# A causal attention and mixture-of-experts kernel: the router's embedding on ScalarE's queue, eleven warming transposes, some low parts on GpSimd, and a new order of steps

## Chip, core and metric

The kernel runs on one core of a Trainium2 chip. The time is the device time of one execution in microseconds (us), and lower is better.

## What is computed

Attention over 48 heads (4 batches of 12, 448 tokens, head width 64) is followed by a mixture of 8 experts on the 1792 tokens that it gives. Each token goes to the one expert with the largest logit.

```python
scores = scale * np.matmul(q, k.transpose(0, 1, 3, 2))
scores = np.where(mask, -1000000000.0, scores)          # causal
attn = softmax(scores); x = attn @ v                    # (4 x 448) x 768
en = expert_emb / (norm(expert_emb) + 1e-06)
logits = xn @ en.T / tau
expert_idx = np.argmax(logits, axis=1)
for e in range(8):
    h = np.maximum(x[mask_e] @ w1[e], 0.0)              # 768 -> 1024
    out[mask_e] = gate_w[mask_e] * (h @ w2[e])          # 1024 -> 768
```

## The kernel before

**Attention.** The heads are taken in 24 pairs (p = 0 to 23), six pairs to a batch. A pair's 448 rows are cut in four chunks of 112. For each pair TensorE makes the scores (steps S0 to S3, S02 for two chunks at once), VectorE masks each chunk and takes its row maximum (M, chunk and head, line 420), ScalarE takes the exponential (E, line 425), TensorE turns the result (T0, T2, T3, line 443), ScalarE or VectorE copies the turned blocks out of the accumulator banks (V0x to V3y, line 447), TensorE multiplies by v (PV0 to PV3), the result is copied (VO) and turned together with the router's product (X), and VectorE scales it into the token rows (XE) and the logits (LE). From pair 1 on GpSimd splits part of q and k into a high and a low part (hi, lo, lines 396 and 397), so that TensorE can use a faster format.

**The router's embedding.** Steps EE, es0 to esA load the embedding (8 x 768) and tau, square it (es0, ScalarE), and take the root by Newton steps on VectorE (es1 and following) to scale it.

**Routing.** After each batch of six pairs the steps R0 to Rc find every token's expert and rank, all on small tiles; q0 to qe sum the squares of the token rows on GpSimd. After batch 2 (pair 17) the most frequent expert, called star, is found (CN, Z0 to Z5, ZR), its w1 is loaded in six pieces (LW0 to LW5), each cast to a high part (W, ScalarE, line 603) and a low part (Wl, line 604: five on GpSimd, one on VectorE), and a first tile of its tokens is gathered (Y, YP, YI, YG).

**The experts.** After the last pair's X the first expert tile begins: F0 to F5 are its first product, HT turns its hidden row, G1 to G6 are part of its second product. Its w2 is loaded (LL), cast (A0 to A7, line 897) and its low parts taken (B0 to B7, line 898). Meanwhile the last batch's routing runs as one chain on VectorE: R0 to R5, R6, N0 to N9, Na to Nc give the place of each token in the expert tiles, TB is the product that collects it (line 942), IG writes the list, and GA gathers the second tile with it (line 626). That tile is turned by xta and xtb (line 672). Then a program of 128-token tiles (body) does the rest; TensorE runs it without a break.

**What sets the order.** One long string, ORDER, lists all attention, routing and first-tile steps. They are issued in that order, and each engine works through its own in that order; a token's `:k` names the bank, `/A`, `/V`, `/G` the engine (ScalarE, VectorE, GpSimd) for a step that may run on either.

Of the kernel before, what the change touches and what calls it, by code (L numbers as in the profile page):

```python
# [41 lines left out]
lo.1 E30.0 T3.0:0 E20.0 LDr.2 M00.0 hi.2 E11.0 M10.1 S02.1:2 M11.1 V3y.0/A V3x.0/V S3.1:1 LDv.0 E00.0 E01.0 E21.0
M01.1 M00.1 T0.0:0 lo.2 M21.1 E21.1 V0y.0/A M20.1 T2.0:2 M30.1 LDr.3 E20.1 V0x.0/A LDr.5 M31.1 V2y.0/V V2x.0/A S02.2:1
T2.1:0 S3.2:2 PV0.0:7 es1.0 E01.1 M31.2 V2y.1/A E31.1 E10.1 M20.2 PV1.0 V2x.1/A E11.1 S1.2:0 M30.2 E00.1 M10.2 PV2.0
M11.2 E30.1 hi.5 PV3.0 T0.1:2 M00.2 E30.2 M01.2 T3.1:0 M21.2 S1.3:1 LDv.1 LDr.4 LDr.6 V0y.1/A V0x.1/A es2.0 es3.0
V3y.1/V es4.0 M10.3 hi.3 V3x.1/A lo.3 S3.3:2 M11.3 es5.0 E31.2 S02.3:0 es6.0 M30.3 E01.2 hi.4 E20.2 T3.2:1 es7.0 M01.3
M20.3 es8.0 M31.3 lo.4 E11.2 PV0.1:6 PV1.1 V3x.2/A PV2.1 M21.3 PV3.1 RC.0/G E21.2 LDv.2 E00.2 es9.0:2 M00.3 E10.2
esA.0 T2.2:2 RC.1/G V3y.2/A VO.0/A T0.2:0 V2y.2/A V0y.2/A V2x.2/V S02.4:1 V0x.2/V LDr.7 X.0:2 M00.4 E01.3 M21.4 S3.4:0
PV0.2:7 E11.3 M01.4 E10.3 E20.3 E31.3 LE0.0 PV1.2 LDv.3 E30.3 LE1.0 XE1.0 M20.4 E00.3 E21.3 XE0.0 PV2.2 M30.4 M31.4
VO.1/V T3.3:1 RC.2/G lo.5 LDv.4 S1.4:0 V3y.3/V M11.4 M10.4 T0.3:2 PV3.2 V0y.3/V V3x.3/A S1.5:1 E20.4 V0x.3/A LDr.8  # L50
T2.3:0 S3.5:2 VO.2/A E21.4 V2y.3/A M10.5 E10.4 M11.5 E11.4 V2x.3/V M30.5 S02.5:1 M31.5 hi.6 lo.6 PV0.3:6 M21.5 M00.5
M01.5 X.1:2 E30.4 E00.4 M20.5 XE1.1 E11.5 E30.5 E01.4 T2.4:0 X.2:1 V2y.4/V LDv.5 E00.5 RC.3/G PV1.3 V2x.4/V XE1.2
LE1.2 E31.4 LE0.1 LDr.9 PV2.3 E01.5 LE0.2 XE0.1 E10.5 PV3.3 LE1.1 T0.4:0 XE0.2 V0x.4/A V0y.4/V T3.4:2 V3y.4/V V3x.4/A
S1.6:1 hi.8 M10.6 M11.6 S3.6:0 M31.6 S02.6:2 hi.7 E20.5 E21.5 M30.6 T0.5:1 PV0.4:7 M01.6 E31.5 M20.6 V0x.5/A M21.6
lo.7 T2.5:0 M00.6 V0y.5/A V2y.5/V T3.5:1 S02.7:2 RC.5/G VO.3/A V2x.5/A RC.4/G LDr.10 lo.8 V3x.5/A V3y.5/A S3.7:0 E01.6
M00.7 E30.6 M01.7 M21.7 E20.6 M20.7 M30.7 X.3:1 M31.7 LE1.3 XE1.3 S1.7:2 M11.7 XE0.3 PV1.4 PV2.4 PV3.4 E10.6 E11.6
LDv.6 E00.6 E21.6 M10.7 LE0.3 PV0.5:6 hi.9 T0.6:1 E31.6 V0y.6/A V0x.6/A LDr.11 VO.4/V T2.6:0 V2x.6/A X.4:2 V2y.6/V
E00.7 T3.6:1 E11.7 S02.8:0 PV1.5 E10.7 V3x.6/A E01.7 LDv.7 V3y.6/A PV2.5 lo.9 XE0.4 LE1.4 M00.8 M01.8 RC.6/G PV3.5
M20.8 XE1.4 LE0.4 E31.7 LDv.8 E00.8 S1.8:2 S3.8:1 M21.8 VO.5/V M11.8 X.5:0 M10.8 T0.7:2 XE1.5 PV0.6:7 E21.7 E21.8
LE0.5 hi.11 M31.8 E10.8 E20.7 PV1.6 E30.7 V0y.7/A LE1.5 V0x.7/V PV2.6 XE0.5 hi.10 E20.8 M30.8 PV3.6 T3.7:0 LDr.12  # L60
T2.7:2 VO.6/V V3x.7/A V3y.7/V V2y.7/A V2x.7/V S3.9:1 S02.9:0 M31.9 M30.9 E30.8 M01.9 E01.8 lo.10 S1.9:2 E31.8 q0.5
M11.9 E11.8 E01.9 PV0.7:7 hi.12 T3.8:1 M10.9 M21.9 X.6:2 R0.5:6 PV1.7 PV2.7 V3x.8/A V3y.8/A E30.9 PV3.7 XE0.6 RC.7/G
T0.8:1 M00.9 q3.5 q2.5 LE1.6 XE1.6 WX.5 q1.5 E31.9 LE0.6 M20.9 VO.7/A V0x.8/V LDr.13 T2.8:2 V0y.8/A V2x.8/A E11.9
E20.9 S3.10:0 V2y.8/V S02.10:1 E21.9 M30.10 M00.10 M01.10 LDv.10 E00.10 RC.8/G S1.10:2 PV0.8:7 M11.10 M31.10 M21.10
PV1.8 PV2.8 LDv.9 PV3.8 E00.9 lo.12 R1.5 E10.9 M20.10 T0.9:0 M10.10 R2.5 lo.11 R3.5 E21.10 S1.11:1 R4.5 X.7:2 M11.11
V0x.9/A LDr.14 qa1.5 M10.11 R5.5 V0y.9/A XE0.7 E30.10 T2.9:0 XE1.7 T3.9:1 V2x.9/A LE1.7 RK.5 LE0.7 V2y.9/A V3y.9/A
V3x.9/V VO.8/A E20.10 S02.11:2 S3.11:0 E31.10 RC.9/V X.8:1 M21.11 M30.11 E01.10 E11.10 M31.11 Rg.5/V hi.14 M01.11
qa0.5 PV0.9:7 M00.11 M20.11 E10.10 qb.5 PV1.9 PV2.9 E21.11 LE0.8 XE0.8 XE1.8 E01.11 T2.10:2 LE1.8 R6.5 E30.11 T0.10:0
V2y.10/V V0y.10/V T3.10:1 V2x.10/A S3.12:2 V3y.10/V V0x.10/A LDr.15 LDv.11 E00.11 M30.12 V3x.10/A S02.12:0 S1.12:1
R8.5 PV3.9 M20.12 E31.11 E11.11 PV0.10:6 M10.12 M11.12 M01.12 hi.13 E20.11 M00.12 qc.5 PV1.10 VO.9/A E10.11 M31.12  # L70
# [1111 lines left out]
```

## Time and profile before

| | us |
|---|---|
| median of 3 runs | 473.37 (473.09 to 474.11) |
| the profiled execution, its own time | 474.17 |
| span in its profile | 472.0 |
| busy: TensorE, VectorE, ScalarE, GpSimd | 454.4, 349.3, 295.9, 158.0 |

The busy time of TensorE is that of a pipelined engine whose ends are modelled, so 96% of the span does not say that TensorE sets the pace everywhere. The stretches up to about 161 us are attention, those behind it the experts.

### The profile page before, as it was taken

The numbers are of one execution on the slowest core, as the hardware profiler recorded it, in microseconds if no ns is written. First come the engines' busy times: TensorE is split into PE (matmuls) and PEld (weight loads), VectorE is DVE, ScalarE is ACT, GpSimd is POOL, SyncE is SP. The second block draws the span as 40 slices with busy tenths as digits, with TensorE's granted clock in tenths as the row PEclk, the third lists the DMA queues.
The fourth block names the chain that finished last, engine by engine and source line by source line (L and its number), as shares of the span: only waits on it lengthen the run. The fifth ranks groups of instructions, "written<-read, shape, count | busy, mean of one in ns | idle before, by whom it ended". The sixth has DMA issues, their size and how long they took to land. (4 is left out here: it accounts for less than half of the span.)

```text
span 472.0 us, 12320 instructions
## 1 busy us (share of the span) xinstructions
PE 454.4 (96%) x3948; PEld 380.9 (81%) x3948; DVE 349.3 (74%) x1024; ACT 295.9 (63%) x731; POOL 158.0 (33%) x158
## 2 busy tenths in 40 slices
...
GB/s 181 206 102 92 169 179 120 138 216 118 150 134 276 269 124 97 69 33 164 174 378 294 296 52 267 76 392 223 301 330 227 110 69 56 284 180 283 286 250 38
DMA packets 27779, 87.35 MB, mean 185 GB/s; under 512 B 2710, under 2 KB 3670, under 8 KB 27680
## 3 DMA queue, kind: packets, MB, share of 16 engines
...
## 5 line engine op out<-in xcount | busy, mean ns | idle before, releaser
L425 ACT ACTIVATE aq<-aq,mx 112x224 f32<-112x224 f32 (+3 forms) x192 | 99.9, 529 | 2.4 <-DVE mx L420 2.3
...
L420 DVE CUSTOM_DVE_ANT_0 aq<-bank,ar 112x224 f32<-112x224 f32 (+3 forms) x192 | 76.0, 441 | 12.1 <-PE bank L415 10.6
L458 PE MATMUL bank<-ap 112*64 112x448 f32 (+3 forms) x384 | 53.2, 409 | 0.0
L721 DVE STREAM_TRANSPOSE turned<-fa 32x256 f32<-32x256 f32 x112 | 48.8, 436 | 1.8 <-DVE akr L733 0.3
L822 ACT COPY fa<-bank 128x512 f32<-128x512 f32 x28 | 15.2, 588 | 54.4 <-PE bank L763 40.3
L626 POOL DMA_INDIRECT fa<-xd,ig x21 | 23.7, 1129 | 62.8 <-PE bank L694 51.2
L443 PEld LDWEIGHTS bank<-idt,aq 64*112 64x112 f32 (+1 forms) x960 | 33.2, 131 | 13.9 <-ACT aq L425 4.4
L1030 DVE TENSOR_TENSOR wl<-fa,wh 128x1024 fp32r<-128x1024 f32 x36 | 41.5, 1218 | 3.1 <-PE bank L764 1.6
L447 ACT COPY ap<-bank 112x384 f32<-112x384 f32 (+2 forms) x91 | 39.5, 474 | 3.2 <-PE bank L443 1.6
L443 PE MATMUL bank<-idt,aq 48*112 48x48 f32 (+1 forms) x960 | 38.6, 219 | 2.3 <-ACT aq L425 1.0
L458 PEld LDWEIGHTS bank<-ap 112*64 112x64 f32 x384 | 23.8, 136 | 20.7 <-issue 12.6
L425 ACT ACTIVATION_READ_ACCUMULATOR aq<-aq,mx 112x1 f32 x192 | 37.8, 197 | 0.0
L1029 ACT CAST wh<-fa 128x1024 fp32r<-128x1024 f32 x36 | 34.9, 1048 | 3.5 <-PE bank L765 1.6
L763 PE MATMUL bank<-wh,akr 128*128 128x512 f32 x84 | 33.0, 393 | 0.0
L765 PE MATMUL bank<-wh,apr 128*128 128x512 f32 x84 | 32.9, 391 | 0.0
L765 PE MATMUL bank<-wh,akr 128*128 128x512 f32 x84 | 32.8, 391 | 0.0
L397 POOL TENSOR_TENSOR wl<-ak,wh 128x672 fp32r<-128x672 f32 x20 | 32.4, 1626 | 1.1
L764 PE MATMUL bank<-wl,akr 128*128 128x512 f32 x84 | 32.8, 391 | 0.0
L764 PE MATMUL bank<-wl,aor 128*128 128x512 f32 x84 | 32.8, 390 | 0.0
L763 PE MATMUL bank<-wh,aor 128*128 128x512 f32 x84 | 32.7, 389 | 0.0
L415 PE MATMUL bank<-ak 64*112 64x224 f32 (+3 forms) x224 | 31.3, 359 | 0.5 <-DVE ar L492 0.3
...
## 6 DMA issues: line engine op xcount, KB each, us to landing
...
```

The source lines that it names most:

```text
L397: step("lo", SPLIT)(lambda p: g.tensor_tensor(los[p % 3], late(p), his[p % 3], op=ALU.subtract))
L420: v.tensor_tensor_reduce(out=Ps[p % 2][i, h], in0=st.pop(("sp", p, i, h)), in1=mask[i], scale=-0.125, scalar=3e38, op0=ALU.add, op1=ALU.mi ...
L425: ac.activation(x, x, AF.Exp, bias=mxs[p % 3][:, h, i : i + 1], scale=-1.0, accum_out=sums[p % 3][:, h, i : i + 1])
L443: pe.transpose(t[:, h, k], Ps[p % 2][i, h][r, c * CP : c * CP + CP], idt[r, r], tile_position=(r.start, 0))
L447: copy()(PTs[p % 2][:, :, slice(*GROUPS[n]), ROWS[half]], st["pt", p, n][half])
L458: pe.matmul(st["o", p][64 * h : 64 * h + 64, CP * c : S], vts[p % 4][:, c, 64 * h : 64 * h + 64], PTs[p % 2][:, h, RUNS[c]], start=c == 0, ...
L721: v.transpose(xk[32 * j : 32 * j + 32, :, q : q + 32], blocks[q : q + 32, :, j])
L763: pe.matmul(acc[j], xh[:, k], wh[k][:, o], start=k == ends[0], stop=False)
L764: pe.matmul(acc[j], xh[:, k], wl[k][:, o], start=False, stop=False)
L765: pe.matmul(acc[j], xl[:, k], wh[k][:, o], start=False, stop=k == ends[1])
L1029: ac.copy(h[k], r[:, k])
L1030: v.tensor_tensor(l[k], r[:, k], h[k], op=ALU.subtract)
```

## The change

The embedding and tau are loaded by ScalarE's queue at the head of the program, in place of SyncE's, and the exponential's table is loaded behind them. Step es1 is cut in two: the guess and one Newton step stay es1 and stand in ORDER ahead of every other VectorE step, and the second Newton step is es1b. The transposes that run on TensorE before the first score go from sixteen to eleven. The low parts Wl and B take their engine from ORDER; there Wl5 stays on VectorE and the other five Wl on GpSimd, as before, and B1, B3, B4 and B7 go to GpSimd. ORDER is new in full: 1246 steps as before, es1b for EE.

```diff
 ORDER = """
-LDa.0 LDr.0 S1.0:1 EE.0 es0.0 S3.0:0 S02.0:2 M11.0 M10.0 M31.0 LDr.1 M30.0 M20.0 M21.0 S1.1:1 M01.0 hi.1 E10.0 E31.0
+es0.0 LDa.0 es1.0 S1.0:1 LDr.0 S02.0:0 M00.0 E00.0 M11.0 M01.0 LDr.1 M10.0 S1.1:2 hi.1 M20.0 M21.0 S3.0:1 M11.1 M30.0
...
         v.memset(es, 0.0)
-        ac.activation(es[:, 5:6], es[:, 5:6], AF.Exp)
...
-        @step("EE", FIRST)
-        def _(p):
-            sy.dma_start(er, emb)
-            sy.dma_start(es[:, 4:5], tau.broadcast_to([E, 1]))
-
+        ac.dma_start(er, emb)
+        ac.dma_start(es[:, 4:5], tau.broadcast_to([E, 1]))
+        ac.activation(es[:, 5:6], es[:, 5:6], AF.Exp)
         step("es0", FIRST)(lambda p: ac.activation(ej, er, AF.Square, accum_out=es[:, 0:1]))
         @step("es1", FIRST)
         def _(p):
             guess = es[:, 2:3].bitcast(I32)
             v.tensor_scalar(guess, es[:, 0:1].bitcast(I32), 1, None, ALU.arith_shift_right)
             v.tensor_scalar(guess, guess, 532487669.0, None, ALU.add)
-            for _ in range(2):
-                for f in newton(es[:, 2:3], es[:, 0:1], es[:, 2:3], es[:, 3:4]):
-                    f()
+            once()
+
+        def once():
+            for f in newton(es[:, 2:3], es[:, 0:1], es[:, 2:3], es[:, 3:4]):
+                f()
+
+        step("es1b", FIRST)(lambda p: once())
...
-            step(f"Wl{k}", STAR)(lambda p, k=k: (g if k < KD - 1 else v).tensor_tensor(l1[k], stage[k % 3], h1[k], op=ALU.subtract))
+            step(f"Wl{k}", STAR)(lambda p, k=k: vg().tensor_tensor(l1[k], stage[k % 3], h1[k], op=ALU.subtract))
...
-            step(f"B{k}", END)(lambda p, k=k: v.tensor_tensor(
+            step(f"B{k}", END)(lambda p, k=k: vg().tensor_tensor(
                 l2[k], r2[:, k], h2[k], op=ALU.subtract))
...
-        for _ in range(16):
+        for _ in range(11):
             pe.transpose(bx[:, :P], idt, idt)
```

ScalarE's first instructions, at the head of the program, before (`es` is the small tile of the norm, `fa` holds the embedding, `aq` the exponentials, `mx` the row maxima):

```order
L261 ACT_TABLE_LOAD
L261 ACTIVATE es<-es 8x1
L348 ACTIVATE fa,es<-fa 8x768
L425 ACTIVATE aq,sum_142<-aq,mx_139 112x224
L425 ACTIVATE aq,sum_142<-aq,mx_139 112x448 x2
L425 ACTIVATE aq,sum_142<-aq,mx_139 112x336
```

and the same place now:

```order
L342 DMA fa<-in_emb_dram 8x768
L343 DMA es<-in_tau_dram 8x1
L344 ACT_TABLE_LOAD
L344 ACTIVATE es<-es 8x1
L345 ACTIVATE fa,es<-fa 8x768
L426 ACTIVATE aq,sum_141<-aq,mx_138 112x112
L426 ACTIVATE aq,sum_141<-aq,mx_138 112x224
```

The two loads stand ahead of the table load, the square (es0) still stands ahead of the first exponential, and the first exponential is that of a chunk of 112 columns instead of 224.

GpSimd's instructions around the end of attention, before (line 604 is Wl, line 469 the first half of RC, line 626 a gather; the last row holds GA and two gathers behind it):

```order
L604 TENSOR_TENSOR wl_75<-fa,wh_74 128x1024
L469 TENSOR_SCALAR sum_143<-sum_143 112x8
L626 DMA fa<-xd,ig_121 128x768
L469 TENSOR_SCALAR sum_142<-sum_142 112x8
L604 TENSOR_TENSOR wl_75<-fa,wh_74 128x1024 x2
L469 TENSOR_SCALAR sum_144<-sum_144 112x8
L604 TENSOR_TENSOR wl_75<-fa,wh_74 128x1024 x2
L626 DMA fa<-xd,ig 128x768 x3
```

and now, from the first tile's gather on (line 605 is Wl, line 899 is B, of 128 x 768):

```order
L627 DMA fa<-xd,ig_120 128x768
L470 TENSOR_SCALAR sum_141<-sum_141 112x8
L605 TENSOR_TENSOR wl_75<-fa,wh_74 128x1024
L470 TENSOR_SCALAR sum_142<-sum_142 112x8
L605 TENSOR_TENSOR wl_75<-fa,wh_74 128x1024
L899 TENSOR_TENSOR aqr<-fa,akr 128x768
L470 TENSOR_SCALAR sum_143<-sum_143 112x8
L605 TENSOR_TENSOR wl_75<-fa,wh_74 128x1024 x2
L899 TENSOR_TENSOR apr<-fa,apr 128x768
L899 TENSOR_TENSOR aqr<-fa,aqr 128x768
L899 TENSOR_TENSOR apr<-fa,apr 128x768
L627 DMA fa<-xd,ig 128x768 x3
```

Four B have come in: B1 behind Wl1, and B7, B3 and B4 between the last two Wl (Wl3, Wl4) and GA, which opens the last row.

VectorE's instructions in the last batch's routing chain, before (line 521 is R5, 487 XE, 604 Wl5, 918 to 923 N0 to N5, 536 R6):

```order
L521 TENSOR_TENSOR O<-bank_72,rmx 112x32
L487 TENSOR_TENSOR fa<-bank_70,R_138 112x4x64
L604 TENSOR_TENSOR wl_75<-fa,wh_74 128x1024
L487 TENSOR_TENSOR fa<-bank_69,R_138 112x4x64
L918 TENSOR_SCALAR ni<-bank_72 112x8
L536 TENSOR_TENSOR pos<-bank_72,O 112x32
L919 TENSOR_SCALAR ni<-ni 112x8
L920 TENSOR_TENSOR te<-ni,star 112x8
L921 TENSOR_REDUCE ts<-te 112x1
L922 TENSOR_TENSOR te<-ni,te 112x8
L923 SCALAR_TENSOR_TENSOR ct<-on_99,te 112x8
```

and now:

```order
L522 TENSOR_TENSOR O<-bank_71,rmx 112x32
L488 TENSOR_TENSOR fa<-bank_70,R_137 112x4x64
L537 TENSOR_TENSOR pos<-bank_71,O 112x32
L488 TENSOR_TENSOR fa<-bank_69,R_137 112x4x64
L919 TENSOR_SCALAR ni<-bank_71 112x8
L488 TENSOR_TENSOR fa<-bank_68,R_137 112x4x64
L545 TENSOR_REDUCE pi<-pos 112x4
L920 TENSOR_SCALAR ni<-ni 112x8
L551 TENSOR_SCALAR t_117<-pi 112x4
L921 TENSOR_TENSOR te<-ni,star 112x8
L922 TENSOR_REDUCE ts<-te 112x1
L923 TENSOR_TENSOR te<-ni,te 112x8
```

Wl5 has left the chain (it stands ahead of R0 now), and one XE more stands in it; the small products keep their order.

Over the whole table the engine of these steps changes: of the copies of 384 elements ScalarE has three more (V0x 19 to 14, V2x 12 to 18, V3y 12 to 14), of 288 four fewer (V0y 15 to 12, V2y 15 to 14), of 512 (V3x) one fewer, of 448 (VO) one more, and VectorE the opposite of each. Of the last products of the star's search R9 (pair 17), Y0 and Y3 go from GpSimd to VectorE, three RC from GpSimd to VectorE, one Rg from ScalarE to VectorE.

## Rows read from the trace of the kernel before

**Rows 1.** Windows: stretch, length; PE, PEld, DVE, ACT, POOL busy (instructions); clock, DMA, GB/s.

```profile
7.06:155.40 148.34, 145.17 (x2132) 105.05 (x2130) 135.62 (x620) 143.53 (x493) 96.92 (x95) 1.00 0.49 161
155.40:161.60 6.20, 6.20 (x98) 4.91 (x98) 5.94 (x15) 5.18 (x11) 3.08 (x3) 1.00 0.67 246
161.60:182.30 20.70, 18.42 (x114) 15.63 (x113) 19.66 (x62) 12.59 (x23) 8.60 (x5) 1.00 0.54 166
182.30:467.00 284.70, 279.00 (x1588) 250.69 (x1586) 187.24 (x324) 132.23 (x203) 45.52 (x38) 1.00 0.55 201
```

**Rows 2.** Waits of ScalarE from 7 to 155.4 us: us, times, longest.

```profile
ACT aq L425 <- DVE mx L420: 2.3, 5, 0.8
ACT ap L447 <- PE bank L443: 1.6, 5, 0.4
```

**Rows 3.** Timeline of the first 8 us: start, us, engine, line.

```profile
0.81 1.28 ACT L261 ACT_TABLE_LOAD   x1 [0.81 <-PEq L1169]
1.44 3.68 PE L1000 MATMUL bank<-idt 128*128 128x128 f32 x16 [1.44 <-POOL idt masks.py:199]
2.20 0.53 SPq L345 DMA_DIRECT2D fa<-in_emb_dram  x1
5.05 1.20 PEld L415 LDWEIGHTS bank<-ak 64*112 64x112 f32 x8 [0.33 <-issue]
5.30 0.84 ACT L348 ACTIVATE fa<-fa 8x768 f32<-8x768 f32 x1 [2.99 <-DMA fa<-in_emb_dram]
6.31 0.39 DVE L420 CUSTOM_DVE_ANT_0 aq<-bank,ar 112x224 f32<-112x224 f32 x1 [5.33 <-PE bank L415]
7.06 0.48 ACT L425 ACTIVATE aq<-aq,mx 112x224 f32<-112x224 f32 x1 [0.83 <-DVE mx L420]
```

**Rows 4.** Timeline: the first and last of the 12 instructions of es1.

```profile
13.59 0.13 DVE L352 TENSOR_SCALAR es<-es 8x1 int32<-8x1 int32 x1
...
15.56 0.14 DVE L325 TENSOR_SCALAR es<-es 8x1 f32<-8x1 f32 x1
```

**Rows 5.** ScalarE's copies by shape, 0 to 190 us: count, busy, mean ns.

```profile
L447 ACT COPY ap<-bank 112x384 f32<-112x384 f32 x43 | 20.3, 479 | 1.4 <-PE bank L443 0.6 <-ACT aq L425 0.3 <-issue 0.3
L447 ACT COPY ap<-bank 112x288 f32<-112x288 f32 x30 | 12.0, 400 | 0.8 <-PE bank L443 0.5 <-DVE ap L447 0.2
L447 ACT COPY ap<-bank 112x512 f32<-112x512 f32 x18 | 10.5, 586 | 1.0 <-ACT aq L425 0.5 <-PE bank L443 0.4
L464 ACT COPY ao<-bank 128x448 f32<-128x448 f32 x17 | 9.1, 534 | 1.0 <-PE bank L458 1.0
```

**Rows 6.** Timeline: VectorE products with two operands in memory, and GpSimd beside them.

```profile
19.34 1.63 POOL L397 TENSOR_TENSOR wl<-ak,wh 128x672 fp32r<-128x672 f32 x1
19.52 1.47 DVE L323 TENSOR_TENSOR es<-es 8x1 f32<-8x1 f32 x1
137.39 5.49 POOL L562 TENSOR_TENSOR fa<-fa 112x768 f32<-112x768 f32 x4
157.49 0.95 DVE L898 TENSOR_TENSOR aqr<-fa,akr 128x768 fp32r<-128x768 f32 x1
161.56 4.77 POOL L604 TENSOR_TENSOR wl<-fa,wh 128x1024 fp32r<-128x1024 f32 x2 [3.03 <-ACT wh L603]
164.51 2.89 DVE L604 TENSOR_TENSOR wl<-fa,wh 128x1024 fp32r<-128x1024 f32 x1
```

**Rows 7.** Timeline from the last batch's first routing step (R0) to the second tile.

```profile
162.15 0.97 DVE L514 TENSOR_REDUCE bank<-ar 112x32 f32<-112x384 f32 x1
171.11 0.66 PE L682 MATMUL bank<-idt,fa 128*128 128x128 f32 x4 [0.62 <-ACT fa L822]
172.20 0.56 PE L942 MATMUL bank<-M,turned 112*128 112x42 f16 x16 [0.43 <-DVE M L936]
174.19 1.98 POOL L626 DMA_INDIRECT fa<-xd,ig  x1 [7.86 <-DVE aqr L685]
179.06 0.87 PE L672 MATMUL bank<-idt,fa 128*128 128x128 f32 x6 [0.98 <-DMA fa<-xd,ig]
```

More of the change, by code (lines that the diff above doesn't have):

```diff
@@ L40 @@
 ORDER = """
-LDa.0 LDr.0 S1.0:1 EE.0 es0.0 S3.0:0 S02.0:2 M11.0 M10.0 M31.0 LDr.1 M30.0 M20.0 M21.0 S1.1:1 M01.0 hi.1 E10.0 E31.0
[L42 to L70, printed above, removed]
@@ L111 @@
-Wl5.17 F1.23 RK.23 WX1.22 F2.23 A4.23 XE1.23 N0.23 R6.23 A1.23 N1.23 N2.23 N3.23 F3.23 Rg.23/A N4.23 N5.23 R7.23 Ra.23
-Q0.23 A5.23 Q1.23 Rb.23 N6.23 N7.23 Wl4.17 F4.23 N8.23 RL0.23 Rc.23 N9.23 F5.23 Na.23 Nb.23 Nc.23 U0.23 B1.23 A0.23
-HTa.23:4 TB.23:2 IG.23 RL1.23 LL3.23 WX2.23 HHa.23 HLa.23 HTb.23:5 U1.23 GA.23 HHb.23 G1.23 G2.23 Q2.23 A6.23 U2.23
-B4.23 HLb.23 A7.23 U3.23 G3.23 IU.23 U4.23 U5.23 G4.23 H0.23 xta.23:3 Q3.23 xtb.23:4 xha.23 H1.23:5 B5.23 G5.23 B6.23
-B7.23 xla.23 B0.23 xhb.23 H2.23 G6.23 xlb.23 IS.23
+es0.0 LDa.0 es1.0 S1.0:1 LDr.0 S02.0:0 M00.0 E00.0 M11.0 M01.0 LDr.1 M10.0 S1.1:2 hi.1 M20.0 M21.0 S3.0:1 M11.1 M30.0
```

114 lines of the change are left out of this document (74 added, 40 removed).

## The prediction

> **What bounds the kernel now.** I read the busy times by stage first [rows 1]. From the first exponential to the last one (7.06 to 155.4 us) ScalarE is busy for 143.53 of 148.34 us, 97%, and VectorE for 135.62, 91%. TensorE shows 98%, but its weight loads fill only 105.05 us of it, so its modelled ends overstate it. Attention goes at ScalarE's pace: its gaps are 4.81 us in all, of which 2.3 us are waits for a row maximum from VectorE and 1.6 us waits for turned blocks from TensorE [rows 2]. From 155.4 us on TensorE does the last pair's products without a break, and from 182.30 to 467.00 us it is busy for 279.00 of 284.70 us, in steps that the change does not touch. What begins earlier at 182.30 us therefore ends earlier by as much, and the question is when the program of 128-token tiles begins. Between F0 (161.60) and that point lie 20.70 us with 18.42 us of TensorE work [rows 1]; the gaps hang on the last batch's routing chain on VectorE, which is itself busy for 19.66 us there. The list product TB waits 0.43 us for that chain, HT (171.11) 0.62 us for a copy on ScalarE, and the second tile's turn 0.98 us for the gather GA that the chain sets off [rows 7].
>
> **The start.** Sixteen transposes run from 1.44 us, and the first score's weights load at 5.05: 3.61/16 = 0.226 us each. Eleven end at 3.92 us. The first score (5.05 to the mask at 6.31) takes 1.26 us, and the new order's next, a chunk of half the columns, about 0.6: scores ready at 5.8 us. The first load's landing isn't shown; it is known to be no later than 5.05, so the gain of this part lies between 0 and 5 x 0.226 = 1.13 us. The new rival for the first mask is the norm. On SyncE the embedding was issued at 2.20 and its square began at 5.30 us, 3.10 later, behind the first two loads [rows 3]. On ScalarE it is issued where the table load begins now, at 0.81; the square begins not before two issues and the table load are through (0.81 + 0.53 + 0.3 + 1.28, and 0.2 for the first small exponential: 3.1 us), and not after 0.81 + 3.10 = 3.9. With its 0.9 us (5.30 to about 6.2 us now, es0 and its sum) and seven VectorE instructions of es1 at (15.70 - 13.59)/12 = 0.176 us [rows 4], 1.23 together, the first mask starts at 5.2 to 6.1 us. I take 5.9, with the scores. From mask to exponential it was 0.75 us for 224 columns; a chunk of 112 needs about 0.6, so the first exponential starts at 6.5 in place of 7.06 us: **-0.6** (0 to -1.1). In the seven instructions moved VectorE saves 1.23 us later, where it is hidden mostly by VectorE's own 12.7 us of gaps; a quarter reaches ScalarE through the 2.3 us of waits: **-0.3** (0 to -1.2). The two issues cost ScalarE about what they cost SyncE, 0.53 us for the first, in time when it only waited (2.99 us ahead of es0), and SyncE's next load goes out earlier by both, which nothing on the way to the first exponential waits for.
>
> The Trainium skill ("Trainium Kernel Development and Optimization", Key Constraints) says that loads issued from several engines run on the same DMA engines, so that a second queue only saves issue time. By that alone the move would be worth nothing beyond SyncE's issue time; the sum above takes its gain from fewer transposes and from the place of es1.
>
> **ScalarE's copies.** Counting the new table: three more of 384 elements, four fewer of 288, one fewer of 512, one more of 448, and one Rg of 0.19 us fewer; by the means [rows 5] 3 x 0.479 - 4 x 0.400 - 0.586 + 0.534 - 0.19 = -0.41 us. One more 384 copy (0.48) stands behind the last exponential than before. Neighbours overlap by about 0.1 us each, on three instructions fewer, so **-0.5** (-0.9 to 0) until the last exponential. VectorE gets the opposite and has the gaps for it.
>
> **Products moved to VectorE in mid-attention.** Here a wait has to be priced. The Newton product at 19.52 us, eight elements, took 1.47 us where es1's instructions take 0.13 to 0.18 [rows 4]: it ends as GpSimd's low part (19.34 + 1.63) does. Wl5 on VectorE took 2.89 us for what a like product needs about 1.1 (B, three quarters as wide, took 0.95): it ends 1.07 us after GpSimd's pair of Wl at 161.56 + 4.77 [rows 6]. So a VectorE product with both operands in memory stands still until GpSimd's running instruction ends. R9, Y0 and Y3 are such products and now run on VectorE while GpSimd squares and halves token rows (5.49 us for four, 1.4 each [rows 6]). Each can stand for 0 to 1.4 us, with the masks queued behind it, and the masks feed ScalarE. Bounds 0 and +4; mostly hidden by VectorE's 9% of gaps: **+0.5**. Three RC on VectorE cost it some 0.2 us each, hidden likewise.
>
> The Trainium skill ("SBUF — State Buffer", SBUF: two separate sides) states this as an exclusive lock: whichever of a two-operand VectorE instruction or a GpSimd instruction starts first holds the shared port for its whole length. The two rows at 19.5 and 164.5 us agree. By this rule the low parts moved to GpSimd do not simply relieve VectorE.
>
> **From attention's end to F0.** Behind the last exponential TensorE had the last pair's turns, X of pair 21, the first tile's turn, PV and two X; now it has T2 and one PV step more before the last pair's PV, and three X behind it instead of two, in place of X of pair 21 ahead. The work is the same within half a microsecond: 0 (-0.4 to +0.4).
>
> **The routing chain.** VectorE loses Wl5 (2.89 us) from the chain and gains one XE. Laid out from F0 = 0 with the present chain's own steps (R0 at 162.15, +0.54, XE behind R5 two us later): R5 ends at about +2.4, R6 and three XE reach N2 at +4.7. With GpSimd silent the rest takes as long as now, and TB could run at +9.6 instead of +10.6, limited by F5 and HT. But GpSimd isn't silent. W3 stands behind the last VO on ScalarE, so Wl3 starts about 1 us before F0; Wl3 and Wl4 at 4.77/2 = 2.4 us, then B7, B3, B4 without a pause. A B on GpSimd is not in the trace; 1.63 us for 672 and 2.39 us for 1024 columns are its bounds, and by columns 768 give 1.8. GpSimd is then occupied until about +9.5, and N2, N4, N5, all with both operands in memory, stand behind B7, B3 and B4 in turn: 1.2 + 1.5 + 1.7 us. TB comes at +13 in place of +10.6, and GA, queued behind B4 and the list, at about +13.9 in place of +12.6. TensorE has work of G1 to G4 to fill the time until the gather lands (174.19 to 179.06, 4.9 us), and H1 and B2 cost it some 0.3. The tile program begins at about +22.1 instead of +20.7: **+1.2** (+1.4 less a little, as a product may catch a gap). If nothing waits, -2.0: the gaps shrink from 2.28 us, and the second tile lands 2 us sooner.
>
> Sum: -0.6 - 0.3 - 0.5 + 0.5 + 1.2 = +0.3 on the profiled execution's own 474.17 us (span 472.0 and 2.17 around it), which is 0.80 above the median. **Forecast 473.5 us**, no change; a run of this kernel tells some 0.2%, or 0.95 us, from nothing.
>
> **The rivals.** *The chain is free* (faster): GpSimd's low parts run at other times than N2 to N5, or the small products slip between them. For it: some 1 us separates N2's place from GpSimd's, and only two stalls of the kind are shown. Against: five GpSimd instructions in a row span the chain. -0.6 - 0.3 - 0.5 + 0.5 - 2.0 = -2.9: 470.5 us. *Attention stalls* (slower): Y0, Y3 or R9 stand behind GpSimd with masks queued, and exponentials run out; ScalarE's gaps grow from 4.8 to 7 us, and with the chain's +1.2 the time is 475.3. It decides once these stalls pass 1.5 us together, for then the start's gain is gone. For it: both engines are over 90% busy. Against: VectorE's 12.7 us of gaps. *The start gives nothing*: the norm lands at 6.1 us or the first load late, and only the rest remains: +1.2 - 0.5 + 0.5 = +1.2 at most, 474.5; this is the change not doing what it says.
>
> **How the numbers follow.** Forecast 0.45, chain free 0.25, attention stalls 0.2, start gives nothing 0.1. The forecast's own range, from its bounds, is 471.8 to 475.2; half of it lies within 0.95 us of the median, a bit over a quarter below. The second rival is nearly always faster (0.9), the third 0.8 slower, the fourth half and half. Faster: 0.45 x 0.28 + 0.25 x 0.9 + 0.2 x 0.03 + 0.1 x 0.2 = 0.38. Same: 0.45 x 0.5 + 0.25 x 0.1 + 0.2 x 0.17 + 0.1 x 0.4 = 0.32. Slower 0.30. The range that leaves out a tenth on each side: 470.2 to 475.8.
>
> **What would show it.** The first exponential between 6.2 and 6.8 us; es1 ahead of the first mask. ScalarE's gaps until the last exponential near 5 us. On VectorE N2, N4 or N5 (lines 921 to 924) with more than 1 us instead of 0.17, each ending with a GpSimd B; TB (line 943) waiting 3 us for VectorE. If these lines show 0.2 us each, the first rival holds. If Y0, Y3 or R9 show over 1 us on VectorE and ScalarE's waits for maxima grow past 4 us, the second does. Wrong altogether would be a gain or loss of TensorE behind 182.30 us, in the tiles.

## The result and the profile after

The changed kernel takes 478.85 us (median of 4 runs, 476.85 to 479.44), the kernel before on the same chip 473.23 us (4 runs, 472.34 to 474.11). The ratio is 1.0111, with an interval of 1.0075 to 1.0147: **slower by about 1.1%**, outside the range of the prediction. The profiled execution of after is the quickest of its four, 476.85 us with a span of 475.1 us, so the rows below show 3.1 of the 5.6 us; what the other runs lost in addition is taken up with the experiments.

The stages of after, as the windows of [rows 1] for before (length; busy time and instructions of PE, PEld, DVE, ACT, POOL; granted clock, DMA share, GB/s):

```profile
7.05:153.60 146.55, 142.89 (x2127) 105.02 (x2127) 137.79 (x622) 142.55 (x490) 95.51 (x89) 1.00 0.50 161
153.60:163.43 9.83, 7.93 (x103) 5.65 (x99) 5.09 (x14) 6.85 (x13) 5.18 (x4) 0.83 0.80 281
163.43:186.74 23.31, 19.98 (x115) 18.22 (x113) 20.69 (x63) 12.69 (x23) 12.84 (x8) 0.85 0.31 95
186.74:470.00 283.26, 278.86 (x1587) 250.21 (x1586) 186.56 (x320) 130.81 (x202) 45.27 (x38) 1.00 0.56 202
```

The two middle stages are longer, 9.83 us for 6.20 and 23.31 for 20.70, and in both the granted clock is below 1.00, which it is in none of the four stages of [rows 1]. Step by step against the forecast, from the times of the first and last exponential, F0, the tile program and the end:

| | before | after | difference | forecast |
|---|---|---|---|---|
| start to first exponential | 7.06 | 7.03 | 0.0 | -0.6 |
| to the last exponential's end | 148.34 | 146.51 | -1.8 | -0.3 (= -0.3 - 0.5 + 0.5) |
| to F0 | 6.20 | 9.89 | +3.7 | 0 |
| to the tile program | 20.70 | 23.31 | +2.6 | +1.2 |
| to the end of the span | 289.7 | 288.4 | -1.3 | 0 |

**The start.** Timeline of after (start, us, engine, line), to set beside [rows 3]:

```profile
3.97 2.59 PE L416 MATMUL bank<-ak 64*112 64x224 f32 x12
5.18 0.14 DVE L324 TENSOR_SCALAR es<-es 8x1 f32<-8x1 f32 x1
6.71 0.27 DVE L421 CUSTOM_DVE_ANT_0 aq<-bank,ar 112x112 f32<-112x112 f32 x1 [1.38 <-PE bank L416]
7.03 0.39 ACT L426 ACTIVATE aq<-aq,mx 112x112 f32<-112x112 f32 x1 [2.95 <-DVE mx L421]
```

TensorE begins the scores 1.08 us sooner than in [rows 3] (3.97 for 5.05) and es1 is through at 5.32, as laid out. But the first mask waits 1.38 us for the scores of the first two steps (S1 and S02, twelve products), which come at 6.6 instead of 5.8 us. The same twelve products in e1 (an experiment below, the same program up to there):

```profile
3.98 1.65 PE L416 MATMUL bank<-ak 64*112 64x224 f32 x12
```

There the first mask starts at 5.78 us and the first exponential at 6.10, sooner than forecast. The twelve take 2.59 us in one execution and 1.65 in the other. The trace's records of the granted clock begin at 7.43 us in after and at 4.54 us in e1 (6.79 before), both with 1.00. What a window shows ahead of the first record is no record, so this difference is put down to the clock by the durations alone.

**Attention's end.** TensorE, and GpSimd's first gather:

```profile
153.05 1.33 PE L444 MATMUL bank<-idt,aq 64*112 64x64 f32 x40
156.27 0.85 PE L673 MATMUL bank<-idt,fa 128*128 128x128 f32 x6 [1.90 <-DMA fa<-xd,ig]
157.05 3.86 PE L459 MATMUL bank<-ap 112*64 112x112 f32 x20
163.43 0.50 PE L764 MATMUL bank<-wh,akr 128*128 128x512 f32 x1
```
```profile
148.38 1.21 POOL L627 DMA_INDIRECT fa<-xd,ig  x1 [0.17 <-issue]
```

and the windows around the wait:

```profile
154.00:156.00 2.00, 0.38 (x14) 0.24 (x10) 1.03 (x3) 2.00 (x5) 1.51 (x1) 1.00 0.82 249
156.00:158.00 2.00, 1.73 (x14) 1.27 (x16) 1.23 (x1) 1.21 (x3) 1.20 (x1) 0.90 0.73 227
158.00:160.00 2.00, 2.00 (x10) 0.79 (x8) 1.02 (x2) 0.80 (x3) 1.14 (x2) 0.50 0.92 334
160.00:162.00 2.00, 2.00 (x30) 1.59 (x28) 0.04 (x1) 1.05 (x2) 0.00 (x0) 0.74 1.02 406
```

In the kernel before, the same two (gather and turn):

```profile
151.29 1.21 POOL L626 DMA_INDIRECT fa<-xd,ig  x1 [0.30 <-DVE ig L621]
157.04 0.88 PE L672 MATMUL bank<-idt,fa 128*128 128x128 f32 x6
```

The turn of the first tile's rows (XTa, line 673) stands ahead of the last pair's PV on TensorE, as it did before, and now waits 1.90 us for the gather YG. TensorE is free for it 5.99 us behind the gather's issue (156.27 - 1.90 - 148.38), where before it took the turn up 5.75 us behind (157.04 - 151.29): the turn has not moved nearer to its gather. The gather lands 7.8 us after its issue, where it took 5.3 before. With 5.3 it would have come at 153.7, ahead of TensorE. In after two loads of weights (512 and 768 KB) go out at 148.25 and 148.83, beside the gather, and its packets move only from 4.45 us behind its issue on; before, such loads went out at 144.5 to 145.8, ahead of it, and its packets moved from 2.36 us on. In thirteen of the fourteen profiles of the new order it took 7.2 to 8.0 us, and 4.2 in e9, where it went out behind the loads. That the loads hold it up is what this suggests; no run moved the loads.

Behind that wait the granted clock goes to 0.50, the level of 1.2 GHz, where [rows 1] has 1.00 for the whole stretch, and the PV behind it takes 3.86 us.

**The routing chain.** VectorE, and under it GpSimd:

```profile
167.69 1.40 DVE L920 TENSOR_SCALAR ni<-ni 112x8 int32<-112x8 int32 x1
169.13 1.76 DVE L921 TENSOR_TENSOR te<-ni,star 112x8 f32<-112x8 int32 x1
171.12 1.57 DVE L923 TENSOR_TENSOR te<-ni,te 112x8 f32<-112x8 int32 x1
172.72 0.17 DVE L924 TENSOR_TENSOR_SCAN ct<-on,te 112x8 f32<-112x8 f32 x1
```
```profile
162.51 4.75 POOL L605 TENSOR_TENSOR wl<-fa,wh 128x1024 fp32r<-128x1024 f32 x2 [3.28 <-ACT wh L604]
167.22 1.85 POOL L899 TENSOR_TENSOR apr<-fa,apr 128x768 fp32r<-128x768 f32 x1
169.02 1.85 POOL L899 TENSOR_TENSOR aqr<-fa,aqr 128x768 fp32r<-128x768 f32 x1
170.83 1.84 POOL L899 TENSOR_TENSOR apr<-fa,apr 128x768 fp32r<-128x768 f32 x1
```

N1, N2 and N4 (lines 920, 921, 923) stand 1.40 to 1.76 us instead of 0.17 and end at 169.09, 170.89 and 172.69, where the three B end (169.07, 170.87, 172.67). What TensorE makes of it, its timeline and then the windows:

```profile
176.04 0.71 PE L943 MATMUL bank<-M,turned 112*128 112x42 f16 x16 [3.33 <-DVE M L937]
178.12 0.52 PE L766 MATMUL bank<-akr,aqr 128*128 128x384 f32 x1
178.44 0.52 PE L764 MATMUL bank<-akr,arr 128*128 128x384 f32 x1
183.98 0.82 PE L673 MATMUL bank<-idt,fa 128*128 128x128 f32 x6
```
```profile
174.00:176.00 2.00, 0.00 (x0) 0.00 (x0) 1.90 (x6) 0.00 (x0) 0.00 (x0) 0.67 0.00 0
176.00:178.00 2.00, 1.96 (x22) 1.96 (x22) 1.93 (x8) 0.28 (x1) 0.17 (x1) 0.50 0.00 0
178.00:180.00 2.00, 2.00 (x8) 2.00 (x7) 1.89 (x8) 2.00 (x6) 1.70 (x2) 0.50 0.00 0
180.00:182.00 2.00, 2.00 (x9) 2.00 (x9) 1.87 (x8) 1.51 (x3) 0.80 (x1) 0.62 0.75 224
```

TB waits 3.33 us where [rows 7] have 0.43, the clock falls to 0.50 in the wait, and the products of G1 then start 0.32 us apart. The second tile's turn at 183.98 no longer waits for its gather, for TensorE itself is late (in [rows 7] it waited 0.98 us at 179.06).

### The profile page after: what moved, and what is told of

Same layout as the page of the kernel before. It is cut to its first block, busy times and chain, and to the rows that moved or that the text cites. A ratio compares the mean times of both kernels' runs of the same rounds, so it can differ in the third digit from the quotient of the medians.

```text
span 475.1 us, 12327 instructions
## 1 busy us (share of the span) xinstructions
PE 455.1 (96%) x3943; PEld 383.1 (81%) x3943; DVE 351.6 (74%) x1028; ACT 295.2 (62%) x729; POOL 163.1 (34%) x156
## 5 line engine op out<-in xcount | busy, mean ns | idle before, releaser
L426 ACT ACTIVATE aq<-aq,mx 112x336 f32<-112x336 f32 (+3 forms) x192 | 100.0, 529 | 3.6 <-DVE mx L421 3.2
L421 DVE CUSTOM_DVE_ANT_0 aq<-bank,ar 112x112 f32<-112x112 f32 (+3 forms) x192 | 76.1, 440 | 3.9 <-PE bank L416 3.1
L459 PEld LDWEIGHTS bank<-ap 112*64 112x64 f32 x384 | 25.2, 139 | 23.8 <-issue 15.1
```

The source lines that it names most:

```text
L421: v.tensor_tensor_reduce(out=Ps[p % 2][i, h], in0=st.pop(("sp", p, i, h)), in1=mask[i], scale=-0.125, scalar=3e38, op0=ALU.add, op1=ALU.mi ...
L426: ac.activation(x, x, AF.Exp, bias=mxs[p % 3][:, h, i : i + 1], scale=-1.0, accum_out=sums[p % 3][:, h, i : i + 1])
L459: pe.matmul(st["o", p][64 * h : 64 * h + 64, CP * c : S], vts[p % 4][:, c, 64 * h : 64 * h + 64], PTs[p % 2][:, h, RUNS[c]], start=c == 0, ...
```

## Experiments

The theory after the result is that two stalls of TensorE cost their wait and then the lower clock behind it: the late gather, and TB behind the locked chain. "Locked" means here that a VectorE instruction stands until GpSimd's running one ends. One rival is that the lock or the order costs alone, without the clock; another is the start. Each group of kernels shared a chip and its runs of the kernel before, and the changed kernel ran only in its own four runs, so a kernel is compared with the changed one by their ratios to before. The groups are e1 to e4 (473.00 us, 13 runs), e5 to e8 (473.78, 25), e9 to e12 (473.09, 23), e13 and e14 (472.95, 17), e15 and e16 (472.99, 23).

**e1, B on VectorE**

```diff
-B1.23/G ... B7.23/G ... B3.23/G ... B4.23/G
+B1.23/V ... B7.23/V ... B3.23/V ... B4.23/V
```

> The changed kernel with B1, B3, B4 and B7 back on VectorE, the order unchanged. Theory (two stalls of TensorE, the gather of the first tile and the routing chain behind GpSimd's low parts, each made longer by TensorE's lower clock level behind it): N1 to N4 fall from 1.4 to 1.8 us to about 0.2 each, the wait of TB from 3.3 to under 0.8 us, the products G1 and G2 run at the full level (0.17 us apart, not 0.32); 3 to 4.5 us faster than the changed kernel, 474.5 to 476. Rival (the new order of attention and its star search is what costs): under 1 us. Rival (only the stall's own length counts, not the clock): about 2.5 us.

477.33 us (473.39 to 480.11, 10 runs), ratio 1.0078 (1.0043 to 1.0113). In the profile TB follows HTa by 0.43 us and the clock is 1.00 from 162 us on, as the theory has it; the fall at 158 to 162 stays. The level is a miss: 3 to 4.5 us were expected, and 477.33 is 1.5 us below the changed kernel's median, between the two rivals (under 1; about 2.5), with intervals that overlap. Two products of the first tile now wait 1.37 and 0.93 us for the B that queue on VectorE, without a fall behind them. The runs were not alike: three with a mean granted clock of 0.995 took 473.4 to 474.3, six of the other seven, at 0.984 to 0.988, 477.1 to 480.1.

**e2, e3, the gather ahead of Wl2, without and with e1's edit.** In both kernels Wl2 comes behind LW5, which loads into the buffer Wl2 reads, so it takes the low part of other rows: part of the first product is changed.

```diff
-Wl2.17/G E11.23 ... LW5.17 ... YG.17 RC.21/G
+E11.23 ... LW5.17 ... YG.17 Wl2.17/G RC.21/G
```

> The changed kernel with the first tile's gather (YG) ahead of Wl2 in GpSimd's order, nothing else. Theory: the gather is issued at about 146.4 instead of 148.4 us, XTa's wait for it falls from 1.9 to under 0.5 us, TensorE stays at its full level in the last pair's PV (2.1 us, not 3.9), F0 starts 3 to 4 us earlier: 475 to 476. Rival (the transfer is held up by the weight loads beside it, whenever it is issued): it lands when it lands now, under 1 us gained.

> Both of the other two edits together. Theory: the gains add, 6.5 to 8.5 us off the changed kernel, 470.5 to 472.5, which is below the kernel before by 1 to 2.5 us, since attention itself ended 1.9 us earlier in the changed kernel. Rival (attention's new order is slower): not below 474.

482.48 us (1.0179, 1.0139 to 1.0219) and 480.85 us (1.0157, 1.0119 to 1.0195). A miss through the edit itself. In e2 Wl2 now waits 3.35 us for LW5's load, the RC queued behind it on GpSimd is late, VectorE waits 4.33 us for that, and PV 3.7. Nor did the gather go out sooner: at 148.97 and 148.35 us, for 148.38 in after, as its list was late too. So these two do not tell what an earlier gather would give.

**e4, idle transposes in the two waits**

```diff
+        step("ZA", END)(lambda p: fill(14, 2))
+        step("ZB", END)(lambda p: fill(24, 5))
-XTa.23:2 ... TB.23:5
+ZA.23 XTa.23:2 ... ZB.23 TB.23:5
```

> The changed kernel with 14 transposes of the identity ahead of XTa and 24 ahead of TB on TensorE, into the banks that these steps overwrite: work that nothing uses, to keep TensorE occupied in its two waits. Theory: both waits stay as long (1.9 and 3.3 us from the end of the work before), but the granted clock stays at 1.00, the last pair's PV takes 2.1 us and the products of G1 and G2 stand 0.17 us apart; 3.5 to 4 us faster, 474.5 to 475.5. Rival (the waits alone cost, the clock's level is a side effect of counting): no faster than the changed kernel, or slower by the overhang of the transposes.

476.82 us (476.17 to 477.44, 4 runs), ratio 1.0085 (1.0068 to 1.0103); the granted clock is 1.00 from 150 to 187 us. TensorE of e4:

```profile
154.90 1.75 PE L1002 MATMUL bank<-idt 128*128 128x128 f32 x14
157.06 0.88 PE L673 MATMUL bank<-idt,fa 128*128 128x128 f32 x6 [0.41 <-DMA fa<-xd,ig]
157.87 2.30 PE L459 MATMUL bank<-ap 112*64 112x112 f32 x20
162.61 0.50 PE L764 MATMUL bank<-wh,akr 128*128 128x512 f32 x1
```

The same PV take 2.30 us, and from XTa to F0 it is 5.55 us where after needs 7.16 (163.43 - 156.27): **1.6 us is the clock's share** at this place. From TB to the tile program it is 185.43 - 175.72 = 9.7 us for 10.7. The two places together give 2.6 us, less than the 3.5 to 4 that were expected, and TB came 0.5 us later behind F0 (13.1 us for 12.6). The time is 2.0 us lower, by the ratios 1.2 us, and the ratio's interval lies within that of the changed kernel: the time by itself shows no gain, the stretches of the trace show the clock's share.

**e5, the last pair's PV ahead of the gathered rows**

```diff
-T2.23:0 ... XTa.23:2 ... XTb.23:3 ... PV3.22 ... XHa.23 XLa.23 PV0.23:6 PV1.23
+T2.23:0 ... PV3.22 ... PV0.23:6 PV1.23 XTa.23:2 XTb.23:3 XHa.23 XLa.23
```

> The changed kernel with TensorE's transposes of the first tile's gathered rows (XTa, XTb) behind the last pair's PV0 and PV1, which need no gathered row. Theory (the late gather stalls TensorE for 1.9 us and the granted clock falls behind that stall): no wait on the gather, granted clock 1.00 from 150 to 172 us, F0 at about 161.5 us where the changed kernel has 163.4; the wait ahead of TB and its fall of the clock stay, so 476 to 477.5 us. Rival (the gathered rows bound F0 whatever TensorE does before): F0 stays at 163 to 163.5 us and the time at 478 to 479 us.

476.24 us (473.98 to 479.59, 12 runs), ratio 1.0050 (1.0023 to 1.0077). XTa (158.22) waits for nothing, the clock is 1.00 from 150 to 172 us, and F0 comes 7.1 us behind the last exponential instead of 9.9. TB waits 3.43 us, with the fall behind it. The rival falls. TensorE of e5:

```profile
158.22 0.88 PE L673 MATMUL bank<-idt,fa 128*128 128x128 f32 x6
174.96 0.72 PE L943 MATMUL bank<-M,turned 112*128 112x42 f16 x16 [3.43 <-DVE M L937]
```

**e6, e4's transposes and e1's B; e7, e5 and e1; e8, sixteen transposes**

```diff
-        for _ in range(11):
+        for _ in range(16):
```

> The changed kernel with idle transposes ahead of XTa and TB (as in e4_fill) and B1, B3, B4 and B7 on VectorE (as in e1_b_vector). Theory: both falls of the clock and the lock are gone, the mean granted clock is 0.994 or more in every run, and the time is 473 to 474.3 us without scatter, like the three runs of e1_b_vector whose mean clock was 0.995. Rival (the scatter of e1_b_vector comes from the start of the program, not from the gather's stall): the times scatter over more than 3 us again.

> The changed kernel with both edits: XTa and XTb behind PV0 and PV1 of the last pair, and B1, B3, B4 and B7 on VectorE; no idle transposes. Theory: no stall of over 1 us between 150 and 185 us, the clock stays at 1.00, F0 at 161 to 162 us, TB within 0.5 us of HTa, the second tile about 20.7 us behind F0, and the time 471.5 to 473.2 us, so the change's other edits are worth 0 to 1.5 us. Rival (what the changed kernel lost was not in these two places): 475 us or more.

> The changed kernel with 16 warming transposes in place of 11. Theory (eleven end before TensorE has its higher rate, so the first scores run at either level from run to run, and the first exponential stood at 6.10, 6.90, 7.03 and 7.81 us in four profiles): the first exponential at 6.9 to 7.2 us, the first scores at the quick rate, and the time within 1 us of the changed kernel's, 477.5 to 479 us, since the two stalls near the end stay. Rival (the loss and the scatter come from the start): 475 us or less, and a scatter under 1.5 us.

e6: 478.96 us (477.62 to 481.30), 1.0111 (1.0082 to 1.0140). e7: 476.73 (473.20 to 479.02, 12 runs), 1.0044 (1.0018 to 1.0070). e8: 476.90 (475.38 to 480.00), 1.0061 (1.0034 to 1.0088). The theory of *two* places missed in e6 and e7. Their profiles show falls elsewhere: at 8 to 12, 135 to 138 and 182 to 186 us in e6, at 12 to 16 and 180 to 183 in e7. In e6 falls are not the whole of it: its two runs with a mean clock of 0.996 still took 477.6 us. With B on VectorE there is hardly a wait left in front of TB, and the 24 transposes themselves stand there:

```profile
172.66 2.78 PE L1002 MATMUL bank<-idt 128*128 128x128 f32 x24
175.28 0.56 PE L943 MATMUL bank<-M,turned 112*128 112x42 f16 x16
```

TB follows HTa by 3.05 us, where it is 0.43 in e1. In e7 the five runs with a mean clock of 0.995 or 0.996 took 473.2 to 475.3, the seven others 476.7 to 479.0. In e7, as in e1, two products of the first tile wait (1.38 and 0.93 us) for B3 and for B6, B5, B4, which now queue on VectorE behind TB; in the kernel before, B2 and B3 stood ahead of F0. In e8 the first exponential came at 6.64 us and the profile has no fall at the start, and the time lies below the 477.5 to 479 of the expectation and above the rival's 475; alone it decides nothing.

**e9, five places mended**

```diff
-R9.5 ... R9.17 ... Y0.17 ... Y3.17 ... B7.23/G ... WX2.23 B3.23/G A5.23 ... B4.23/G
+R9.5/G ... R9.17/G ... Y0.17/G ... Y3.17/G ... B7.23/V ... B2.23 B3.23/V ... B4.23/V
```

(with e5's and e8's edits; R9.5, on VectorE in the kernel before as well, goes to GpSimd too)

> The changed kernel with all five places mended at once: 16 warming transposes; R9, Y0 and Y3 on GpSimd as before; XTa and XTb behind PV0 and PV1 of the last pair; B3, B4 and B7 on VectorE, B3 right behind B2; B1 alone stays on GpSimd. Theory (the loss is stalls of TensorE at these places and the granted clock that falls behind some of them): no fall of the clock in any run, a spread under 1.5 us, 472.5 to 473.8 us, so the rest of the change is worth about nothing. Rival (other places of the new order lose as well): over 475 us, or a spread of 3 us or more as in the runs with one or two places mended.

481.20 us (480.80 to 483.75, 5 runs), ratio 1.0178 (1.0147 to 1.0208): both miss. GpSimd, VectorE and TensorE of e9:

```profile
145.34 0.59 POOL L614 TENSOR_TENSOR y<-tf,tok 112x12 f16<-112x12 f32 x1 [0.54 <-DVE tf L612]
145.90 3.56 POOL L563 TENSOR_TENSOR fa<-fa 112x768 f32<-112x768 f32 x3
149.49 0.35 DVE L572 TENSOR_REDUCE n<-fa 112x4 f32<-112x192 f32 x1 [2.81 <-POOL fa L563]
149.76 2.03 DVE L470 TENSOR_SCALAR sum<-sum 112x8 f32<-112x8 f32 x1
153.09 1.83 PE L416 MATMUL bank<-ak 64*112 64x448 f32 x4 [5.12 <-DVE mx L421]
```

With Y3 (line 614) on GpSimd the halvings of the squared rows behind it (line 563) are late, and VectorE's sum of them (line 572) waits 2.81 us with masks behind it. An RC behind that (line 470) then stands 2.03 us under GpSimd's next low part, and TensorE waits 5.12 us for a mask. For Y3 this speaks for VectorE in the new order, where it took 0.17 us in after; the lock that VectorE met there (R9 and Z2, 1.70 and 1.53 us) is shorter than these waits. Which of the three products makes the loss was not tried apart.

**e10, e11, e12: one part each in the kernel before.** e10 gives B1, B3, B4 and B7 to GpSimd at their old places; e11 takes the edits of the start alone; e12 moves one step:

```diff
-W1.17 LE1.20 YG.17 LDv.23 ... VO.22/V Wl2.17 V0x.23/A
+W1.17 LE1.20 LDv.23 ... VO.22/V Wl2.17 YG.17 V0x.23/A
```

> The kernel before with B1, B3, B4 and B7 on GpSimd and every step at its old place. Theory (the products on GpSimd cost where they run under the small products of the routing chain): in the old order none of the four stands ahead of N5, so TB stays within 0.6 us of HTa; B1 stands ahead of GA on GpSimd and may put the second tile's gather 1 to 2 us later: 473.5 to 475.5 us. Rival (the engine of these products alone makes the loss): 476 us or more, with TB 3 us behind HTa.

> The kernel before with the edits at the start alone: embedding and tau from ScalarE's queue, the table load behind them, es0 and one half of es1 ahead of everything on their engines, 11 transposes in place of 16; the rest of the order as before. Theory (the early scores only reach the next stall, the one for the second load, and the granted clock falls behind it in some runs): the first exponential at 6.1 to 7.1 us, no gain in the median, runs between 473 and 476 us, those with a lower mean clock the slower ones. Rival (the start gives what was predicted of it): 472 to 472.8 us without scatter.

> The kernel before with one step moved: the first tile's gather (YG) behind the low part Wl2 on GpSimd, which delays its issue by about 2.5 us from 151.3. Theory (a late gather costs its wait and then the lower clock): the rows land at about 159 to 160 us, TensorE waits 2 to 3 us, the granted clock falls to about 0.5 for some 4 us behind the wait in the runs that are slow, F0 4 to 5 us later, and the time 476 to 479 us. Rival (the wait alone costs, or the landing is not tied to the issue): the granted clock stays at 1.00 and the time is 473.5 to 475.5 us.

e10: 474.49 us (473.66 to 475.68, 12 runs), 1.0031 (1.0017 to 1.0045), inside the theory's range. One detail missed: N1 stands 1.29 us and TB waits 1.56, with a fall at 173 to 177 us. e11: 473.59 us (472.11 to 476.26), 1.0008 (0.9986 to 1.0030), no difference from before that these runs can tell: **the start alone shows no gain**. The 0.9 us forecast for it (-0.6 - 0.3, a ratio of 0.998) lie outside the interval. In its profile the first exponential comes at 6.11 us, 0.95 sooner than before, and F0 at 161.66 (161.61 before): the head start is gone by F0. e12: 476.25 us (475.93 to 476.66, 6 runs), 1.0064 (1.0043 to 1.0085). TensorE of e12 and two windows:

```profile
159.20 0.85 PE L672 MATMUL bank<-idt,fa 128*128 128x128 f32 x6 [1.95 <-DMA fa<-xd,ig]
165.37 0.50 PE L763 MATMUL bank<-wh,akr 128*128 128x512 f32 x1
```
```profile
160.00:162.00 2.00, 2.00 (x11) 0.86 (x12) 1.73 (x5) 0.62 (x2) 0.00 (x0) 0.68 0.98 399
162.00:164.00 2.00, 2.00 (x18) 1.46 (x16) 0.58 (x1) 0.68 (x2) 0.00 (x0) 0.50 0.42 170
```

The gather goes out 2.79 us later (154.08 for 151.29), TensorE waits 1.95 us, the clock falls behind it, and from the turn to F0 it takes 6.17 us in place of 4.57 (161.61 - 157.04, before): again 1.6 us for the clock. F0 is 3.8 us later and the time 3.2 us longer. Here the gather is late because it goes out late (it lands 5.0 us after its issue); in the changed kernel it is late because it takes 7.8 us. The stall is of the same length, and so is its price. So one late gather, in an order otherwise unchanged, costs more than half of the changed kernel's loss; the rival, a wait without a fall, does not hold.

**e13, e14: the two places again.** e13 is e5's edit, B4 and B7 on VectorE and B3 there right behind B2; e14 adds 14 idle transposes near the start.

```diff
-B7.23/G ... WX2.23 B3.23/G A5.23 ... B4.23/G
+B7.23/V ... B2.23 B3.23/V ... B4.23/V
+LDr.0 ZS.0 S02.0:0
```

> The changed kernel with two places mended and nothing else: XTa and XTb behind PV0 and PV1 of the last pair, and B3, B4 and B7 on VectorE with B3 right behind B2; B1 stays on GpSimd, R9, Y0 and Y3 on VectorE, 11 warming transposes. Theory (these two stalls and the clock behind them are the loss): the stall of 5.1 us that e9_repaired had at about 147 us is gone; runs whose clock does not fall at the start take 472.3 to 473.5 us, those where it falls there 475 to 476 us, the median 473 to 475 us. Rival (the new order loses elsewhere too): no run under 474 us.

> The kernel of e13_two_places with 14 idle transposes ahead of S02.0, where TensorE waits up to 2 us for the second load. Theory (the stall at the start lets the granted clock fall in some runs, which makes the scatter): the granted clock is 1.00 from 4 to 30 us in every run, the times lie within 1.5 us of each other, at 472.3 to 473.8 us. Rival (the scatter has another place): a spread of 3 us or more as in e7_pv_vector.

e13: 476.79 us (472.69 to 479.17, 12 runs), 1.0061 (1.0032 to 1.0091). Three runs, all with a mean clock of 0.996, took 472.7 to 472.9; the median missed, and the other nine have lower mean clocks (0.980 to 0.993). Windows of its profiled execution, one of the longer ones:

```profile
14.00:16.00 2.00, 2.00 (x20) 1.95 (x16) 1.31 (x9) 2.00 (x8) 1.73 (x2) 0.52 0.48 159
136.00:138.00 2.00, 2.00 (x23) 1.49 (x22) 1.93 (x6) 1.48 (x6) 1.88 (x2) 0.50 0.00 0
182.00:184.00 2.00, 2.00 (x10) 1.90 (x9) 0.53 (x2) 0.79 (x2) 0.08 (x1) 0.50 0.00 0
```

There are three falls. The first comes behind three waits near the start (1.27 us for the second pair's load, then 1.01 and 0.98); e1 had 1.57, 1.01 and 0.98 there and no fall. The second comes behind 0.9 us for Os, the counts that R9 sums and CN reads, and the third behind 1.9 us for the low parts B6, B5, B4. e14: 475.10 us (474.85 to 476.34, 6 runs), 1.0053 (1.0038 to 1.0067): five of six lie within 1.1 us, no fall ahead of 178 us in its profile, and the third fall remains, so its level is above the expectation.

**e15, e16: all places closed, e16 without the start.** Both build on e13: B4 stands ahead of B6 and B5, and 8 idle transposes (ZC) ahead of CN; e15 also has 14 (ZS) ahead of S1.1.

```diff
-B6.23 B5.23 B4.23/V ... CN.17:6 ... S1.1:2
+B4.23/V B6.23 B5.23 ... ZC.17 CN.17:6 ... ZS.0 S1.1:2
```

> The kernel of e13_two_places with B4 ahead of B6 and B5 on VectorE, 14 idle transposes ahead of S1.1 (where TensorE waits for the second pair's load) and 8 ahead of CN (the wait for Os at 134 us). Theory (every stall left that lets the granted clock fall is closed): the granted clock stays at 1.00 from 4 us to the experts' end in all runs, the spread is under 1.5 us, and the time is 471.5 to 473.3 us, the same as before or 1 us less. Rival (the new order loses elsewhere or the stalls come back at the next place): 474 us or more, or a spread of 3 us.

> The kernel of e15_filled without the idle transposes at the start. Theory: the stall at the start alone decides between two kinds of run: those with a mean clock of 0.996 at 471.5 to 473.3 us, and those with a fall at 8 to 18 us some 2 us longer; a spread of 2 to 3 us. Rival (the start is not what scatters): the same times as e15_filled.

e15: 473.25 us (471.69 to 475.03, 12 runs), 1.0005 (0.9990 to 1.0019); mean clock 0.993 or more in all runs, and in its profile none of the falls of the other kernels. The level is the theory's; the spread of 3.3 us is not, so falls of the kind above do not make this scatter (the mean clock does not hold the time ahead of the first record, 11.18 us in its profile). TensorE at e15's start:

```profile
7.87 3.25 PE L1000 MATMUL bank<-idt 128*128 128x128 f32 x14 [1.30 <-DVE mx L421]
11.04 1.43 PE L416 MATMUL bank<-ak 64*112 64x224 f32 x8
```

Here the idle transposes waited for a bank, took 3.25 us and put the second pair's scores at 11.04 us (7.20 in e1). e16, without them: 472.31 us (471.69 to 475.03, 12 runs), 0.9997 (0.9981 to 1.0013), nine of twelve runs between 471.7 and 472.7. The two kinds of run are not told apart by their mean clock, as was expected: 0.992 and 0.998 both stand among the nine. In its profile the first record of the clock stands at 10.83 us and the first exponential at 7.35, and that run took 472.06 us: a slow start costs little. Its profiled execution begins the tile program at 181.15 us (182.32 before) with a span of 469.9 (472.0). A median 0.7 us below before's, but the interval holds 1: not shown to beat it. It does remove the changed kernel's whole loss (interval 0.9981 to 1.0013 against 1.0075 to 1.0147).

## Why the prediction was wrong

The step that failed is **"From attention's end to F0 ... 0 (-0.4 to +0.4)"**: it counted TensorE's work and not what that work waits for. The gather went out 2.9 us earlier than before and still came too late. It took 7.8 us to land for 5.3 before, beside two loads of weights and with DMA 0.98 to 0.99 busy at 150 to 154 us, while the turn of its rows stood as far behind its issue as before (5.99 us, 5.75 before). TensorE waited 1.90 us, where the step had no wait. Measured were +3.7 us, of which 1.6 are the clock's by e4, as e12 found in the order of the kernel before. Why the gather took 2.5 us longer is not shown beyond the loads beside it. The second omission is that **the clock behind a stall was priced nowhere**, neither here nor in the routing chain, where the plan had TensorE wait 3 us for VectorE.

- *Start, -0.6:* 0.0 in after. The norm landed as laid out; the step "scores ready at 5.8 us" failed, as the first twelve products took 2.59 us. In e1 they took 1.65, and in e1 and e11 the first exponential came at 6.10 and 6.11 us. So the gain depends on the rate at which TensorE runs in the first microseconds of an execution, and by e11 it doesn't reach F0: in e1 TensorE then stood until the next load came at 7.2 us.
- *es1 and ScalarE's copies, -0.3 and -0.5; products on VectorE, +0.5:* with the start's second -0.3 these add up to -0.3, and -1.8 was measured up to the last exponential. ScalarE is busy for 142.55 us, 1.0 less. The rest is partly a matter of where the end is marked: in e16, without stalls, that stretch is 1.0 us shorter and the one to F0 0.9 longer. The lock in mid-attention came for R9, with 1.70 us over its bound of 1.4, and for Z2 (1.53 us, 0.17 before), which the prediction does not name; Y0 (0.25) and Y3 (0.17) did not stand. TensorE waited 0.9 us for Os behind it.
- *Routing chain, +1.2:* right in mechanism, too small. TB came at F0 + 12.6 (forecast +13), GA at +14.4 (+13.9), the tile program at +23.3 (+22.1). The chain was held by N1, N2 and N4, not N2, N4 and N5; 1.0 us of the missing 1.2 (1.4 in the table, since the forecast took 0.2 off) is the clock by e4's TB stretch. A B on GpSimd took 1.85 us, as forecast (1.8).
- *Behind the tile program, 0:* -1.3 in this pair of executions; in all eighteen profiles the stretch is 288.3 to 289.7 us, so it is the scatter of an execution, with before at its upper end.
- *Rivals:* "the chain is free" is refuted by the chain's rows, "the start gives nothing" came true as a part, "attention stalls" did not (ScalarE's gaps are 4.0 us, 4.8 before). None held a falling clock.
- *The sum:* +0.3 on the median of 473.37 gives 473.7, not 473.5; against 478.85 that changes nothing.

The Trainium skill ("TensorE: Matmul & The Clock Gate", Why this matters for your kernels) advises against gaps between matmul bursts since the clock falls back in them. This trace agrees in direction: waits of 1.9 and 3.3 us brought 0.50, and in e4, where transposes filled most of them, it stayed at 1.00.

What stays open is what the three longer runs of the changed kernel (478.4 to 479.4 us) lost beyond the profiled one. Their mean clocks are 0.987, 0.981 and 0.985, the profiled one's 0.986, so more falls are possible for the one at 0.981 (479.26 us) and not shown for the other two; no profile of such a run of this kernel exists. Nor is it known what decides whether a wait is followed by a fall: behind the wait of 0.9 us for Os there was one in e6 and e13, and none in after, e1, e7 and e14. Whether loads of weights moved away from the gather would bring it back to 5.3 us was not tried.
